# Attention with mixed-in projections: projections that end in period 51 instead of 48, head stacks loaded 16 rounds ahead instead of 20, the rounding of a finished projection moved to the end of a period, and all low weight parts made by GpSimd

## The chip, the core and the metric

The kernel runs on one core of a Trainium2 chip. The metric is the device time of one launch in microseconds (us). The core has five engines with queues of their own: TensorE (PE in the profile; PEld is its weight load), VectorE (DVE), ScalarE (ACT), GpSimd (POOL) and SyncE (SP), which issues most of the DMA transfers. Each engine works through its instructions in the order in which the program gives them, and waits where an input isn't there or a buffer isn't free.

## The reference

Four layers on x of 2048 tokens by 576 features: attention, a spectral filter, attention, a spectral filter. The change lies in the two attention layers, which are the same but for their inputs:

```python
def _A_ref(x, wqkv, wo):
    B, S, D = x.shape
    H = 32; Dh = D // H; W = 256
    qkv = (x @ wqkv).reshape(B, S, 3, H, Dh).transpose(2, 0, 3, 1, 4)
    q, k, v = qkv[0], qkv[1], qkv[2]
    scores = jnp.einsum("bhqd,bhkd->bhqk", q, k) * (Dh ** -0.5)
    idx = jnp.arange(S)
    mask = (idx[:, None] - idx[None, :] >= 0) & (idx[:, None] - idx[None, :] < W)
    scores = jnp.where(mask[None, None], scores, -1e9)
    p = _softmax(scores, axis=-1)
    o = jnp.einsum("bhqk,bhkd->bhqd", p, v)
    return o.transpose(0, 2, 1, 3).reshape(B, S, D) @ wo

x = x + _A_ref(_layernorm(x), A_wqkv, A_wo)
x = x + _B_ref(_layernorm(x), B_w_r, B_w_i)   # filter by rfft2 and irfft2
```

So there are 32 heads of 18 features, and each token sees itself and the 255 tokens before it.

## The kernel before

**Precision.** Every product is taken with operands split into a high part, rounded to fp32r, and a low remainder. That is why the code has pairs such as `wh` and `wl`, and why a projected q or k is written out as two parts.

**Projections.** The 1152 columns of q and k are nine blocks of 128 (`i`), and the 2048 tokens four chunks of 512 (`c`). One block with one chunk is a *unit*: 14 steps of matmul (`k_steps`). In the mixed part each step is two matmuls, one on each half of PE's rows, into two PSUM banks `pj` and `pk`. When a unit's last step is done, four things follow: ACT copies both banks into an SBUF tile `sg` (line 1129); `total` adds them on POOL (line 1133); `high` rounds the sum on ACT (line 1136); `remainder` takes the low part on POOL (line 1142); and `send` stores both parts, 512 KB, in the DRAM tensor `qk_d` with a DMA from SP's queue (line 1145). There are two `sg` tiles, taken in turn.

**Stacks.** The heads are done in eight groups of four (`n`, `NQ = 8`). A group's q and k stand in SBUF as a *stack*: two tiles `qs` and `ks`, which hold the parts in slots one above the other so that one matmul gives the sum of the products. Even groups use one pair of tiles and odd groups the other. `stack_load` (line 1162) fills one chunk of 512 tokens of a stack from `qk_d`, and a quarter of a chunk takes three DMAs of 72 KB. The quarters 0 and 1 fill `qs`, 2 and 3 `ks`.

**Rounds and periods.** One round `t` handles one tile of 128 keys or queries of one group, for its four heads; 16 rounds are a group and 128 rounds the layer. Ten rounds ahead (`LEAD = 10`) the maximum of each query's scores is found: a matmul `S` (line 1187) and one DVE instruction with the mask, followed by a short read of its accumulator (line 1189). In `m_rows` four tiles' maxima are turned by PE (`tpm`, line 1199), negated by ACT (`mt`, line 1201) and put by two small DMAs of SP (line 1203) into a spare row of `qs`; the matmul `E` (line 1219) then gives scores that are already lowered by the maximum, and ACT takes their exponential into `P` (line 1220). Two selects of POOL (lines 1222 and 1225) clear what the mask excludes.

Two rounds are a *period* `p`, and `mixed()` writes 59 of them (`MIX = 118`). A period has first its block of eight `S` and eight `E` matmuls with the projection steps between them, and at its end the *value block*: 32 small matmuls `U` of `P` with v (line 1240; 16 of them where a group begins), which DVE then transposes (line 1246). Ahead of the value block stand the actions planned in `end`; odd periods also have an `m_rows` behind it. Even periods have a transpose `back` (line 1270) and odd ones a reciprocal (line 1261) on DVE. `early` actions are written behind the first `S` of a period, `mid` actions after its first round. A `U` shares three PSUM banks with the `E` matmuls, so it takes over the bank of the sixth `E` of its period and starts only when ACT is done with that one.

**What sets the order.** All of it is written out by hand. `ends` says in which period each of the 23 units of the mixed part is finished (the earlier ones are done in an opening part): with `1 + 47 * u // 22` in periods 1 to 48, most of them two periods apart and seven steps in each. Periods that have no step are filled with 14 small matmuls on an identity (`warmpj`, `warmpk`). `loads(t)` says which quarter of which stack is loaded in round `t`.

**Weights of the next product.** In the last periods (`behind`) the output weights are loaded in five pieces, and `out.split(k)` makes the high part on ACT (line 751) and the low part by a subtraction (line 752): on POOL for the first three pieces and on DVE for the last two. `OB` is 120.

After period 58 a short tail does the remaining ten rounds (exponentials and values only), and then the product with the output weights begins.

## Time and profile before

| what | us |
|---|---|
| median of three runs | 1326.73 |
| lowest and highest run | 1315.5, 1673.2 |
| the profiled execution: its time | 1323.85 |
| the profiled execution: its span (first to last instruction) | 1322.1 |
| first attention layer, value block of period 1 to that of period 49 | 249.22 |
| second attention layer, the same stretch | 247.44 |

The page gives for each engine its busy time, for each group of instructions the count, the mean time of one and the idle time ahead of it with what ended it, and the chain of work that ended last. The answers of the trace that are shown below are of these kinds: busy time by stretch; a timeline of one engine, in which a row gives the start in us, the duration, the engine, the line, the instruction with its tiles and shapes, and in square brackets the idle time ahead of it and what ended that. SPq is SyncE's queue of DMA issues. A row whose last column is x4 stands for four instructions in a row.

### The profile page before, as it was taken

What the parts mean: (1) busy time and instruction counts of PE and PEld (TensorE: products, weight loads), DVE (VectorE), ACT (ScalarE), POOL (GpSimd) and SP (SyncE); (2) the same over time, 40 slices, a digit from 0 to 9 for tenths busy, and PEclk for the clock granted to TensorE, in tenths of its full rate; (3) what the DMA queues carried; (4) which work ended last, traced back from release to release, by engine and by line L of the source; (5) the groups of instructions that cost most, each with busy time, mean ns of one, the idle gap of its engine ahead of it and who ended that gap; (6) DMA issues with size and microseconds to landing.
All of it is one profiled execution on the core that took longest, in us unless ns stands there. A gap on an engine that the chain in (4) does not pass through costs nothing.

```text
span 1322.1 us, 35482 instructions
## 1 busy us (share of the span) xinstructions
PE 1281.5 (97%) x12115; PEld 1005.3 (76%) x12115; DVE 956.0 (72%) x3196; ACT 777.0 (59%) x1944; POOL 771.0 (58%) x1248
## 2 busy tenths in 40 slices
PE   8999999999999899999999999999999999899998
PEld 8986666666678699975999976666666686897687
DVE  5417889889899577757674148888889896676755
ACT  5522777878777545533355315777877778473233
POOL 2258777898776443567221196788878767113811
PEclk9999999999999999999999999999999999999999
DMA  6846666665566646688873368576665667498874
GB/s 202 220 153 206 209 199 219 213 213 193 192 199 218 199 120 225 198 261 258 275 264 74 89 204 224 194 212 195 199 199 184 201 207 247 137 346 266 287 237 164
DMA packets 179497, 274.37 MB, mean 208 GB/s; under 512 B 67743, under 2 KB 77727, under 8 KB 177989
## 3 DMA queue, kind: packets, MB, share of 16 engines
q1 hardware_dynamic: 167007, 243.63, 58.7%
q0 software_dynamic: 4656, 13.44, 3.8%
q10 hardware_dynamic: 7654, 15.03, 3.2%
q8 instruction: 97, 1.59, 0.5%
q14 instruction: 83, 0.68, 0.2%
HBM read 164.54 MB, written 114.81 MB: 211 GB/s over the span
## 4 chain that ended last, share of the span: by engine, by line
PE 80%; ACT 6%; DMA 5%; DVE 4%; issue 2%; SPq 1%; POOL 1%; DVEq 0%; ACTq 0%; POOLq 0%
PE U L1240 11%; PE pj L1115 10%; PE vps L1005 9%; PE S L1187 8%; PE ops L802 7%; PE pk L1115 6%; PE E L1219 6%; PE po L274 4%; ACT P L1220 4%; PE pq L524 3%; PE p L503 2%; PE pf L274 2%; PE pi L600 2%; PE pz L312 1%; DMA ks<-qk_d 1%
## 5 line engine op out<-in xcount | busy, mean ns | idle before, releaser
L1189 DVE CUSTOM_DVE_ANT_0 jk<-S,mask 128x384 bf16<-128x384 f32 (+2 forms) x1024 | 482.8, 527 | 35.1 <-PE S L1187 13.3
L1220 ACT ACTIVATE P<-E 128x384 f32<-128x384 f32 (+2 forms) x1024 | 409.3, 487 | 95.4 <-PE E L1219 49.7
L1219 PE MATMUL E<-qs,ks 64*128 64x384 f32 (+2 forms) x1024 | 324.3, 372 | 7.2 <-ACT P L1220 4.5
L1187 PE MATMUL S<-ks,qs 63*128 63x384 f32 (+2 forms) x1024 | 325.0, 370 | 5.6 <-DMA qs<-qk_d 2.7
L1222 POOL TENSOR_SCALAR_AFFINE_SELECT P<-P 128x512 f32<-128x512 f32 x256 | 162.3, 634 | 133.5 <-ACT P L1220 125.3
L1219 PEld LDWEIGHTS E<-qs,ks 64*128 64x128 f32 x1024 | 180.6, 185 | 63.1 <-ACT P L1220 42.1
L1187 PEld LDWEIGHTS S<-ks,qs 63*128 63x128 f32 x1024 | 172.7, 185 | 66.0 <-DVE m L1189 37.8
L1240 PE MATMUL U<-P,vq 128*32 128x256 f32 (+2 forms) x3840 | 185.1, 329 | 0.0
L1240 PEld LDWEIGHTS U<-P,vq 128*32 128x32 f32 (+1 forms) x3840 | 107.1, 109 | 75.4 <-POOL P L1225 16.3
L1115 PE MATMUL pj<-xh,wqh 64*128 64x512 f32 (+1 forms) x360 | 154.9, 430 | 0.0
L1225 POOL TENSOR_SCALAR_AFFINE_SELECT P<-P 128x512 f32<-128x512 f32 x224 | 144.0, 643 | 0.0
L1115 PE MATMUL pj<-xh,wql 64*128 64x512 f32 (+1 forms) x360 | 138.6, 425 | 0.0
L1115 PE MATMUL pj<-xl,wqh 64*128 64x512 f32 (+1 forms) x288 | 120.4, 418 | 0.0
L802 PE MATMUL ops<-oroom 128*128 128x290 f32 (+1 forms) x812 | 114.0, 297 | 1.7 <-DVE ofree L848 1.2
L802 PEld LDWEIGHTS ops<-oroom 128*128 128x128 f32 x812 | 110.4, 189 | 2.3 <-ACT ofree L836 1.5
L1115 PE MATMUL pk<-xh,wqh 64*128 64x512 f32 x230 | 92.2, 401 | 0.0
L1115 PE MATMUL pk<-xh,wql 64*128 64x512 f32 x230 | 91.1, 400 | 0.0
L1246 DVE STREAM_TRANSPOSE us<-U 128x256 f32<-128x256 f32 x128 | 57.1, 446 | 46.6 <-PE U L1240 45.6
L1189 DVE DVE_READ_ACCUMULATOR2_ANT m<- 128x1 f32 x1024 | 84.9, 83 | 0.0
L1115 PE MATMUL pk<-xl,wqh 64*128 64x512 f32 x184 | 73.1, 397 | 0.0
L1115 PEld LDWEIGHTS pj<-xh,wqh 64*128 64x128 f32 (+1 forms) x360 | 66.8, 186 | 7.5 <-issue 1.5
L789 POOL TENSOR_TENSOR oroom<-oraw,oroom 64x128 fp32r<-64x128 f32 x26 | 13.9, 535 | 99.1 <-ACT oroom L787 49.2
(522 smaller groups left out, 2869.6 us busy)
## 6 DMA issues: line engine op xcount, KB each, us to landing
qk_d<-sg SPq DMA_DIRECT2D x56, 512.0 KB
qs<-qk_d SPq DMA_DIRECT2D x384, 72.0 KB
ks<-qk_d SPq DMA_DIRECT2D x348, 72.0 KB
op_d<-o SPq DMA_DIRECT2D x56, 256.0 KB
v_d<-vt SPq DMA_DIRECT2D x32, 304.0 KB
vq<-v_d SPq DMA_DIRECT2D x16, 608.0 KB
wt<-in_w SPq DMA_DIRECT2D x16, 580.0 KB
ofree<-x SPq DMA_DIRECT2D x16, 580.0 KB
```

Source lines behind the costliest of these rows:

```text
L274: T.matmul(ps[:, c, 0:NF], tail[r] if si == 4 else hl_(si), dcs[b // 2][r, b % 2], start=mi == si == 0, stop=si == 4)
L802: self.nc.tensor.matmul(self.ps[u][n][:, 0:self.n], x, self.w[p][:, (2 * wk + n) * self.n:(2 * wk + n + 1) * self.n], start=first and i == ...
L1005: T.matmul(ps[:, n, 0:288], xT(xk, c), w[:, wk, n * 288:(n + 1) * 288], start=i == 0, stop=i == len(ks) - 1)
L1115: T.matmul(ps.rearrange("r (n p) -> r n p", n=NT) if second else ps, w[r, wk], x[r], start=s == 0, stop=s == len(ks) - 1)
L1187: T.matmul(ps[:, 0:N], q[b:b + 63, pair, i * 128:i * 128 + 128], k[b:b + 63, pair, lo:hi], start=True, stop=True)
L1189: V.tensor_tensor_reduce(out=jk[:, 0:N], in0=ps[:, 0:N], in1=mask[:, 384 - N:384], scale=1.0, scalar=-3e38, op0=ALU.add, op1=ALU.max, accu ...
L1219: T.matmul(ps[:, 0:nq], k[b:b + 64, pair, j * 128:j * 128 + 128], q[b:b + 64, pair, j * 128:j * 128 + nq], start=True, stop=True)
L1220: A.activation(p[:, hl_, 0:nq], ps[:, 0:nq], AF.Exp, scale=SC)
L1222: P.affine_select(out=p[:, :, 0:128], in_=p[:, :, 0:128], pattern=[[0, 4], [1, 128]], compare_op=ALU.is_ge, fill=0.0, base=0, channel_mult ...
L1225: P.affine_select(out=p[:, :, 256:384], in_=p[:, :, 256:384], pattern=[[0, 4], [-1, 128]], compare_op=ALU.is_gt, fill=0.0, base=0, channel ...
L1240: T.matmul(U[32 * h:32 * h + v.shape[1], (q0 - e) * 128:(q1 - e) * 128], v, pt[n, j][:, h, (q0 - j) * 128:(q1 - j) * 128], start=j == max( ...
L1246: V.transpose(us[n, c][:, 8 * k:8 * k + 8].rearrange("r b (a p) -> r (b a) p", a=2), U[:, 0:256].rearrange("r (p n) -> r n p", n=NT))
```

## The change

Four edits, in `split`, `loads`, `mixed` and `behind`:

- The units end by `1 + 50 * u // 22`: in periods 1 to 51, so that periods 0 to 51 hold steps instead of 0 to 48. Six units take three periods where three did before, and seven periods of a layer have the filling matmuls instead of ten.
- From round 4 on, one quarter of a stack is loaded in each round: the stack that is next, chunk by chunk. Before, stack 2's first chunk was loaded in rounds 12 to 15 beside the last chunk of stack 1, and from then on everything came four rounds earlier than now. The number of loads is the same.
- `high` goes from the middle of the period after the unit's end to the end of that period, ahead of the value block. `remainder` goes from that middle to the beginning of the next period, and `send` from the middle of that next period to its end.
- All five low weight parts are made by POOL, and every split comes two rounds earlier.

```diff
     def split(self, k):
         c = slice(2 * self.n * k, 2 * self.n * (k + 1))
         self.nc.scalar.copy(self.w["h"][:, c], self.raw[:, c])
-        (self.nc.vector if k > 2 else self.nc.gpsimd).tensor_sub(self.w["l"][:, c], self.raw[:, c], self.w["h"][:, c].bitcast(F32))
+        self.nc.gpsimd.tensor_sub(self.w["l"][:, c], self.raw[:, c], self.w["h"][:, c].bitcast(F32))
...
-                n, c = divmod(t + (12 if t < 16 else 20), NT)
-                if 4 <= t < 16 or 1 < n < NQ and t >= 12:
-                    stack_load(1 if t < 16 else n, t // 4 if t < 16 else c // 4, (t % 4,))
-                if 12 <= t < 16:
-                    stack_load(2, 0, (t % 4,))
+                n, c = divmod(t, NT)
+                if t >= 4 and n + 1 < NQ:
+                    stack_load(n + 1, c // 4, (t % 4,))
...
-                ends = [1 + 47 * u // 22 for u in range(23)]
+                ends = [1 + 50 * u // 22 for u in range(23)]
...
                     for total, high, remainder, send in ended:
                         total()
-                        for f in (high, remainder):
-                            plan(mid, p + 1, f)
-                        plan(mid, p + 2, send)
+                        plan(end, p + 1, high)
+                        plan(early, p + 2, remainder)
+                        plan(end, p + 2, send)
...
-                if 0 <= t - (OB - 10) < 10 and t % 2 == 0:
-                    out.split((t - (OB - 10)) // 2)
+                if t - OB + 12 in range(0, 10, 2):
+                    out.split((t - OB + 12) // 2)
```

How the instructions stand on two engines shows the edits best. The first place is ACT in period 4 of the first layer, the period after a unit's end: `P_8` and `P_9` are the exponentials of the period's two rounds, `CAST sg` is `high`. Before:

```order
L1201 ACTIVATE mt_3_1991<-tpm_3_1989 16x128
L1220 ACTIVATE P_8_2002<-E_0_2003 128x384
L1220 ACTIVATE P_8_2002<-E_1_2014 128x384
L1220 ACTIVATE P_8_2002<-E_2_2017 128x384
L1220 ACTIVATE P_8_2002<-E_3_2026 128x384
L1136 CAST sg_2_1960<-sg_2_1960 128x512
L1220 ACTIVATE P_9_2048<-E_0_2049 128x384
L1220 ACTIVATE P_9_2048<-E_1_2058 128x384
L1220 ACTIVATE P_9_2048<-E_2_2061 128x384
L1220 ACTIVATE P_9_2048<-E_3_2070 128x384
```

The same place in the changed kernel, down to the first exponential of period 5:

```order
L1201 ACTIVATE mt_3_1991<-tpm_3_1989 16x128
L1220 ACTIVATE P_8_2002<-E_0_2003 128x384
L1220 ACTIVATE P_8_2002<-E_1_2014 128x384
L1220 ACTIVATE P_8_2002<-E_2_2017 128x384
L1220 ACTIVATE P_8_2002<-E_3_2026 128x384
L1220 ACTIVATE P_9_2046<-E_0_2047 128x384
L1220 ACTIVATE P_9_2046<-E_1_2056 128x384
L1220 ACTIVATE P_9_2046<-E_2_2059 128x384
L1220 ACTIVATE P_9_2046<-E_3_2068 128x384
L1136 CAST sg_2_1959<-sg_2_1959 128x512
L1220 ACTIVATE P_10_2109<-E_0_2110 128x384
```

The rounding moved from behind the fourth exponential of its period to behind the eighth.

The second place is SP's queue in periods 5 to 7 of the first layer, from one pair of `mt` rows to the next: `qs_1059` and `ks_1061` belong to stack 1, `qs_1058` and `ks_1060` to stack 2, `op_d<-o` stores finished values. Before:

```order
L1203 DMA qs_1059<-mt_0_2213 2x4x128 x2
L1162 DMA qs_1059<-qk_d 18x2x512 x3
L1162 DMA qs_1058<-qk_d 18x2x512 x3
L1162 DMA qs_1059<-qk_d 18x2x512 x3
L1162 DMA qs_1058<-qk_d 18x2x512 x3
L1162 DMA ks_1061<-qk_d 18x2x512 x3
L1162 DMA ks_1060<-qk_d 18x2x512 x3
L1275 DMA op_d<-o_1_2309 128x512
L1145 DMA qk_d<-sg_3_2182 128x2x512
L1162 DMA ks_1061<-qk_d 18x2x512 x3
L1162 DMA ks_1060<-qk_d 18x2x512 x3
L1203 DMA qs_1059<-mt_1_2445 2x4x128 x2
```

The same stretch in the changed kernel:

```order
L1203 DMA qs_1059<-mt_0_2213 2x4x128 x2
L1162 DMA qs_1059<-qk_d 18x2x512 x6
L1162 DMA ks_1061<-qk_d 18x2x512 x3
L1275 DMA op_d<-o_1_2301 128x512
L1162 DMA ks_1061<-qk_d 18x2x512 x3
L1145 DMA qk_d<-sg_3_2181 128x2x512
L1203 DMA qs_1059<-mt_1_2433 2x4x128 x2
```

Between the two pairs of `mt` rows stand 12 loads instead of 24, and the send has gone from ahead of the last `ks` loads to directly ahead of the `mt` rows.

## The prediction

> **What bounds the kernel now.** I read the page's head and the chain of work that ended last, then the busy time by stretch of the mixed part, then the timelines of TensorE, ScalarE and SyncE's queue at the places that the diff touches.
>
> ```profile
> span 1322.1 us, 35482 instructions
> PE 80%; ACT 6%; DMA 5%; DVE 4%; issue 2%; SPq 1%; POOL 1%; DVEq 0%; ACTq 0%; POOLq 0%
> ...
> core 0: us, PE busy (x) PEld busy (x) DVE busy (x) ACT busy (x) POOL busy (x), PEclk, DMA share, GB/s
> 136.68:385.90 249.22, 244.53 (x2878) 163.93 (x2876) 219.84 (x863) 193.64 (x484) 201.52 (x282) 0.99 0.64 205
> 385.90:425.91 40.01, 39.66 (x598) 32.89 (x596) 36.67 (x145) 28.15 (x73) 26.84 (x42) 1.00 0.64 200
> 813.60:1061.04 247.44, 244.03 (x2878) 163.37 (x2877) 219.63 (x863) 193.32 (x484) 197.40 (x274) 1.00 0.65 199
> ```
>
> The chain puts 80% on PE, but a busy PE is not PE at its peak. The windows run from value block to value block. The first and third cover periods 2 to 49 of the two attention layers, the second the eight periods 50 to 57 without a projection step. Those eight need 40.01 us, 5.00 a period, with DVE busy for 36.67 of it: eight score maxima a period and the transposes around them bound a period that has nothing else to do. The 48 periods before need 5.19 and 5.16 each. So the whole of what the projections cost in time is 249.22 - 6 x 40.01 = 9.2 us in the first layer and 7.3 in the second, and more if periods 50 to 57 have costs of their own (they do, below).
>
> Which periods pay it? The value blocks give each period's length; the pieces are periods 24, 38 with 39, and 52 with 53.
>
> ```profile
> 253.73 1.51 PE L1240 MATMUL U<-P,vq 128*32 128x256 f32 x32
> 258.85 1.51 PE L1240 MATMUL U<-P,vq 128*32 128x256 f32 x32
> ...
> 324.82 1.51 PE L1240 MATMUL U<-P,vq 128*32 128x256 f32 x32
> 330.17 1.51 PE L1240 MATMUL U<-P,vq 128*32 128x256 f32 x32
> 335.03 1.51 PE L1240 MATMUL U<-P,vq 128*32 128x256 f32 x32
> ...
> 395.03 1.51 PE L1240 MATMUL U<-P,vq 128*32 128x256 f32 x32
> 400.13 1.51 PE L1240 MATMUL U<-P,vq 128*32 128x256 f32 x32
> 405.02 1.51 PE L1240 MATMUL U<-P,vq 128*32 128x256 f32 x32
> ```
>
> Even periods carry a transpose more than odd ones, so I compare like with like. Period 24 has seven steps and ends a unit: 258.85 - 253.73 = 5.12. Period 52 has no step: 5.10. Period 38 also has seven steps, and the rounding of the unit that ended in 37: 5.35. Of the odd ones, 39 has seven steps and a unit's end and lasts 4.86, and 53 has nothing and lasts 4.89. Steps and unit ends thus cost about nothing; the period with the rounding costs 0.25. ScalarE's timeline shows how (period 38, then 52):
>
> ```profile
> 325.10 0.66 ACT L1129 COPY sg<-pj 128x512 f32<-128x512 f32 x1
> 325.57 0.69 ACT L1129 COPY sg<-pk 128x512 f32<-128x512 f32 x1
> ...
> 326.98 1.64 ACT L1220 ACTIVATE P<-E 128x384 f32<-128x384 f32 x4
> 328.49 0.63 ACT L1136 CAST sg<-sg 128x512 fp32r<-128x512 f32 x1
> 328.99 1.67 ACT L1220 ACTIVATE P<-E 128x384 f32<-128x384 f32 x4
> 332.12 1.35 ACT L1220 ACTIVATE P<-E 128x256 f32<-128x256 f32 x4 [1.46 <-PE S L1187]
> ...
> 397.25 3.47 ACT L1220 ACTIVATE P<-E 128x384 f32<-128x384 f32 x8 [0.20 <-PE E L1219]
> ```
>
> The cast splits eight exponentials that otherwise run in one piece of 3.47 us, so the sixth, on whose bank the value block waits, is half a microsecond later: two of the last four, 0.84 us, behind 328.99 is 329.83, and the block starts at 330.17. Behind the eighth exponential ACT then has nothing to do for 1.46 us.
>
> **The change part by part.** *Rounding to the period's end.* The cast of 0.63 us goes into that idle 1.46 us, behind the eighth exponential, where nothing of the value block waits for it. There are 23 units in each layer: 46 x 0.25 = 11.5 us. Bounds: no gain, if the delay comes from something that moves along, and all the excess that the windows leave. For that upper end the weights' own cost in periods 50 to 57 has to be taken off: three of those periods hold a copy of 0.7 us in the middle of ACT's exponentials, like the cast, and if each costs 0.3 the bare eight periods are 39.1; 48 of them are 234.6, so the excess without the stall below is 11 us a layer, 22 in all. I take 11.5, which two pairs of rows give directly.
>
> *Remainder and send.* POOL's subtraction keeps its length and moves half a period back:
>
> ```profile
> 330.19 1.28 POOL L1142 TENSOR_TENSOR sg<-sg 128x512 fp32r<-128x512 f32 x1
> ...
> 321.34 0.39 SPq L1145 DMA_DIRECT2D qk_d<-sg  x1
> ...
> 326.86 1.06 SPq L1203 DMA_DIRECT2D qs<-mt  x2
> ```
>
> Behind it on POOL stand the selects of the next round; the value block needs them only a period later, so 1.28 us is hidden; without that cover it would show 46 times. The send moves past three `ks` loads in SP's queue and stands right ahead of the `mt` rows in odd periods. In before it is issued 5.5 us ahead of them, in the change after the remainder, which by my estimate is done 2.5 us into the period (its 1.28 us behind what POOL has left over from the period before), so about 3 us ahead. I cost this at nothing and keep the late `mt` as a rival. The Trainium skill ("DMA: Bandwidth & Descriptors", section "Queues, rings and completion order") says that each DMA engine takes the descriptors of one ring in their order, which would put the small `mt` rows behind all 512 KB of the send; what that would give here is worked out in that rival.
>
> *Loads, one quarter a round.* Rounds 12 to 15 issue half as many loads. What the doubling costs shows in period 9 of each layer:
>
> ```profile
> 157.32 2.43 SPq L1162 DMA_DIRECT2D ks<-qk_d  x3
> ...
> 161.44 4.46 SPq L1162 DMA_DIRECT2D qs<-qk_d  x12
> 165.94 2.95 SPq L1162 DMA_DIRECT2D ks<-qk_d  x6
> ...
> 171.08 3.00 SPq L1162 DMA_DIRECT2D ks<-qk_d  x6
> 174.18 1.49 SPq L1203 DMA_DIRECT2D qs<-mt  x2
> ...
> 163.64 1.51 PE L1240 MATMUL U<-P,vq 128*32 128x256 f32 x32
> ...
> 173.85 1.51 PE L1240 MATMUL U<-P,vq 128*32 128x256 f32 x32
> 176.95 0.41 PE L1187 MATMUL S<-ks,qs 63*128 63x384 f32 x1 [1.59 <-DMA qs<-qk_d]
> 177.61 0.41 PE L1219 MATMUL E<-qs,ks 64*128 64x384 f32 x1 [0.26 <-DMA qs<-mt]
> 182.39 0.86 PE L1240 MATMUL U<-P,vq 128*32 128x256 f32 x16
> ...
> 850.56 1.51 PE L1240 MATMUL U<-P,vq 128*32 128x256 f32 x32
> 857.11 0.86 PE L1240 MATMUL U<-P,vq 128*32 128x256 f32 x16
> ```
>
> SP's queue is so far behind that the last loads of stack 1 are issued until 174.08 and its maxima until 175.67; PE waits for both. Period 9 lasts 182.39 - 173.85 = 8.54 us in the first layer and 6.55 in the second, against 4.86 for an odd period like it: 3.7 + 1.7 = 5.4 us, which go with the 12 extra loads. Bounds 0, if the queue stays behind, and 5.4; I take all, since the removed issues (half of 4.46, 2.95 and 3.00) are 5.2 us of SP's time.
>
> From stack 2 on, each quarter comes four rounds later: the last quarter of a chunk is issued three rounds ahead of its first use. Stack 1 runs so already: its `ks` loads end at 159.75 and are used behind the value block that ends at 165.15, 5.4 us later; PE's wait at 176.95 says that a load lands within 2.9 us of its issue. Cost nothing, with 2.5 us to spare.
>
> *Steps over three more periods.* The steps are the same and cost 0.02 a period by 24 against 52; 84 filling matmuls a launch fall away where the bound is DVE. Nothing.
>
> *Weights on POOL.*
>
> ```profile
> 429.70 0.79 DVE L752 TENSOR_TENSOR oroom<-ofree,oroom 128x576 fp32r<-128x576 f32 x1 [0.32 <-ACT oroom L751]
> ...
> 420.40 1.41 POOL L752 TENSOR_TENSOR oroom<-ofree,oroom 128x576 fp32r<-128x576 f32 x1
> ...
> 420.81 0.56 DVE L1189 CUSTOM_DVE_ANT_0 jk<-S,mask 128x384 bf16<-128x384 f32 x1
> ...
> 435.44 0.67 ACT L751 CAST oroom<-ofree 128x576 fp32r<-128x576 f32 x1
> ```
>
> In period 58 DVE, the bound there, stops for 0.32 + 0.79 = 1.1 us; on POOL the same costs 1.41 of an engine that is busy for 26.84 of 40.01. The fifth copy leaves the tail, where ACT works without a break (about 0.6), and a copy appears in period 54 (about -0.3). At best 1.4 us a layer, at worst a loss of 0.3 if POOL is late with its selects; I take 1.0, so 2 in all. The Trainium skill ("GPSIMD Engine Reference", section "Engine selection") speaks against the move: it rates POOL at about half DVE's speed with two inputs, and the trace agrees, 1.41 to 0.79. The same page's "Key points" has POOL and DVE contend for SBUF when DVE reads two SBUF inputs; the score maximum at 420.81, wholly inside a POOL subtraction, takes 0.56 like others, so the rule does not bite on an instruction with one input from PSUM.
>
> Sum: 11.5 + 5.4 + 0 + 0 + 2 = 18.9 us. The profiled execution took 1323.85, 1.75 more than its span; less 18.9 that is 1305. It lies 2.9 under the median of the runs (1326.73) and inside their spread, the lowest being 1315.5.
>
> **The rivals.**
>
> *All of the excess goes.* Then the first term is its upper end, 22: 1323.85 - 22 - 5.4 - 2 = 1294. For it: periods 39 and 53 show that steps alone are free. Against: splitting the next block's weights puts copies of ACT into the middle of five other periods, and these stay.
>
> *The rounding was not the cause.* PE ends the chain in this part, so the 0.25 might be PE's. Then 7.4 us remain: 1316. Against: period 24 has as many steps and lacks the 0.25.
>
> *Late maxima.* Issued at 326.86 for 1.06 us, `mt` is needed at 331.68, when the block of 330.17 ends: 3.8 us after the second issue. In period 9, right behind 432 KB of loads, it took from 175.67 to 177.61, 1.9. If the send's 524 KB came wholly ahead of it, at the 205 GB/s of the window that is 2.6 us more, 0.7 too late; in the 12 units that end in odd periods, twice: 17 us, so 1322. Against: 3 us of lead.
>
> *Slower: late stacks.* If SP's queue falls behind by more than 2.5 us, the last quarter lands after its use and PE stands, as in period 9. There are 24 chunks a layer in stacks 2 to 7. A wait of 0.4 us at each of the 48 eats the whole gain; the 1.59 of period 9 would make 76 us, 1381; 1 us makes 1353, which is over 2% slower. For it: three rounds of lead instead of seven, with sends ahead in the queue. Against: stack 1 does well with that lead up to round 12.
>
> **How the numbers follow.** The forecast, 1305, has 0.60; all of the excess 0.16; not the cause 0.13; late maxima 0.05; late stacks 0.06. The forecast's own range is 1298 to 1312. Below 1294 and above 1318 I leave out less than 2 in 10: half of the last two cases and a little of the first two. About 2% is what a measurement of this kernel can tell from no change. Faster by that means under 1300: the second case and a tenth of the first, with runs that spread by 1%, 0.24. Slower by that needs late stacks of over 1 us: 0.04. The rest, 0.72, is within 2%.
>
> **What would show it.** Right: the cast stands behind eight unbroken exponentials in the idle time ahead of the next period; period 38's length falls to about 5.10; period 9 to about 4.9, with no wait of `S` for a load; no subtraction of weights on DVE. Wrong: value blocks still 5.35 apart in the periods after a unit's end; `E` waiting for `mt` in odd periods; `S` waiting for `qs` or `ks` at the start of a chunk; ACT idle ahead of the cast, waiting for POOL's sum.

## The result and the profile after

| | before | after |
|---|---|---|
| median of 18 runs each, us | 1324.45 | 1311.88 |
| lowest and highest run | 1315.5, 1673.2 | 1305.8, 1316.8 |
| the profiled execution: its time | 1323.85 | 1312.47 |
| its span | 1322.1 | 1310.7 |

The run of 1673.2 us lies far outside the others and has no trace; the ratio compares fast runs, so it is not in it.

The ratio is 0.9904 with an interval of 0.9888 to 0.992: a gain of 12.6 us, under the 2% that was set as the bound. The forecast was 1305, a gain of 18.9, with a range of 1298 to 1312. The median lies inside that range by 0.1 us, much less than the runs scatter: that it lies inside at all is luck.

The head of the page of the changed kernel and its chain of work that ended last:

```profile
span 1310.7 us, 35140 instructions
...
PE 81%; DMA 9%; DVE 3%; ACT 2%; issue 2%; SPq 1%; POOL 1%; ACTq 0%; DVEq 0%; POOLq 0%
```

ACT went from 6% of the chain to 2%, and DMA from 5% to 9%: something now stands at transfers. The busy time by stretch of the changed kernel says where; its columns are those of the same view in the prediction (length of the stretch, then PE, PEld, DVE, ACT and POOL busy, clock, DMA share, GB/s). The stretches are cut at the same value blocks as there (periods 2 to 49, then 50 to 57), the first two in the first layer, the others in the second:

```profile
134.64:378.15 243.51, 239.14 (x2832) 161.81 (x2831) 217.80 (x863) 194.18 (x480) 200.05 (x279) 0.99 0.64 205
378.15:420.40 42.25, 39.80 (x561) 31.02 (x559) 36.83 (x146) 30.16 (x78) 30.89 (x45) 1.00 0.75 229
806.09:1045.57 239.48, 237.64 (x2833) 159.76 (x2831) 217.35 (x863) 194.19 (x480) 195.72 (x271) 1.00 0.64 200
1045.57:1090.02 44.45, 40.99 (x561) 32.50 (x559) 36.88 (x145) 30.47 (x77) 31.36 (x45) 0.96 0.74 221
```

The 48 periods are 5.7 us shorter in the first layer (249.22 before) and 8.0 in the second (247.44). But the eight periods behind them, which took 40.01 us in the first layer before, now take 42.25 and 44.45.

**What went as forecast.** Here are the value blocks that bound period 38 and period 9 of the first layer in the changed kernel:

```profile
318.81 1.51 PE L1240 MATMUL U<-P,vq 128*32 128x256 f32 x32
323.93 1.51 PE L1240 MATMUL U<-P,vq 128*32 128x256 f32 x32
...
173.61 1.51 PE L1240 MATMUL U<-P,vq 128*32 128x256 f32 x32
178.51 0.86 PE L1240 MATMUL U<-P,vq 128*32 128x256 f32 x16
```

Period 38, which holds a rounding, lasts 323.93 - 318.81 = 5.12 us instead of 5.35. Period 9 lasts 4.90, in the second layer 4.92 (842.96 to 847.88), instead of 8.54 and 6.55. ScalarE's timeline of period 38 shows the cast where the prediction put it:

```profile
320.96 1.64 ACT L1220 ACTIVATE P<-E 128x384 f32<-128x384 f32 x4
322.76 1.74 ACT L1220 ACTIVATE P<-E 128x384 f32<-128x384 f32 x4 [0.16 <-PE E L1219]
324.37 0.63 ACT L1136 CAST sg<-sg 128x512 fp32r<-128x512 f32 x1
```

The eight exponentials run without the cast between them, and the cast starts when the value block has already begun. The periods that hold a rounding can be compared with periods that hold none and stand at the same place of their group of eight. Summed over the 44 of them outside period 2, the time above such a period was 13.6 us before and is 1.7 after.

**What did not.** TensorE's timeline from the value block of period 56 to that of 57, first layer, then second; and VectorE's in the second layer:

```profile
412.91 1.51 PE L1240 MATMUL U<-P,vq 128*32 128x256 f32 x32
416.53 0.41 PE L1187 MATMUL S<-ks,qs 63*128 63x384 f32 x1 [2.12 <-DMA ks<-qk_d]
...
420.40 0.86 PE L1240 MATMUL U<-P,vq 128*32 128x256 f32 x16
...
1080.33 1.51 PE L1240 MATMUL U<-P,vq 128*32 128x256 f32 x32
1085.13 0.49 PE L1187 MATMUL S<-ks,qs 63*128 63x384 f32 x1 [3.29 <-DVE us L1246]
...
1090.02 0.86 PE L1240 MATMUL U<-P,vq 128*32 128x256 f32 x16
...
1083.93 0.71 DVE L1270 STREAM_TRANSPOSE o<-us 128x512 f32<-128x512 f32 x1 [2.90 <-DMA op_d<-o]
```

Period 57 lasts 7.49 us in the first layer and 9.69 in the second, 5.24 in both before. In the first layer PE waits for the last loads of `ks`, those of chunk 3 of stack 7. In the second DVE waits for a store: `o` has one buffer, `back` writes it, and the store that was to empty it has not landed. The transpose of `U` stands behind `back` on DVE, and PE behind that. SyncE's queue in periods 53 to 56 of the first layer shows the place where both come from; the last row is that of the same loads in the second layer:

```profile
397.46 0.46 SPq L1145 DMA_DIRECT2D qk_d<-sg  x1
...
400.54 0.35 SPq L758 DMA_DIRECT2D dc<-dcr  x1
402.81 1.01 SPq L1162 DMA_DIRECT2D qs<-qk_d  x3
403.86 0.36 SPq L744 DMA_DIRECT2D ofree<-in_wo  x1
...
405.77 1.07 SPq L1162 DMA_DIRECT2D ks<-qk_d  x3
407.49 0.36 SPq L744 DMA_DIRECT2D ofree<-in_wo  x1
407.94 0.72 SPq L1275 DMA_DIRECT2D op_d<-o  x1
408.70 2.68 SPq L1162 DMA_DIRECT2D ks<-qk_d  x3
...
1080.07 1.54 SPq L1162 DMA_DIRECT2D ks<-qk_d  x3
```

The last send of the layer goes out at 397.46, in round 107. The loads of round 108 read what it stores: SP stands from 400.89 to 402.81. Two pieces of the weights (288 KB each by the list of DMA issues; one of the expectations below calls them 580 KB) and a second one of the constants (290 KB each) go out among the loads. The store of `o` goes out at 407.94 and lands by 414.77, when `back` starts. The last three `ks` loads begin to go out at 408.70, are issued by 411.38, and have landed by 416.53: 7.8 us behind the first issue and 5.2 behind the last. The prediction had reckoned with 2.9 behind the last. In the second layer they are issued by 1081.61, when the block of period 56 is nearly over (1081.84).

The same happened once in the middle of a layer. Period 21 of the first layer, where chunk 1 of stack 3 is first used, lasts 7.22 us instead of 5.30:

```profile
230.26 1.02 SPq L1162 DMA_DIRECT2D ks<-qk_d  x3
...
235.49 0.41 PE L1187 MATMUL S<-ks,qs 63*128 63x384 f32 x1 [1.65 <-DMA ks<-qk_d]
```

No weights are on the way there; a load of values (608 KB, issued at 222.98) and a send (512 KB, at 224.54) are.

### The profile page after: what moved, and what is told of

Same layout as the page of the kernel before. It is cut to its first block, busy times and chain, and to the rows that moved or that the text cites. A ratio compares the mean times of both kernels' runs of the same rounds, so it can differ in the third digit from the quotient of the medians.

```text
span 1310.7 us, 35140 instructions
## 1 busy us (share of the span) xinstructions
PE 1269.4 (97%) x11947; PEld 997.1 (76%) x11947; DVE 948.1 (72%) x3192; ACT 781.8 (60%) x1944; POOL 777.3 (59%) x1252
## 4 chain that ended last, share of the span: by engine, by line
PE 81%; DMA 9%; DVE 3%; ACT 2%; issue 2%; SPq 1%; POOL 1%; ACTq 0%; DVEq 0%; POOLq 0%
PE pj L1115 12%; PE U L1240 11%; PE vps L1005 9%; PE S L1187 8%; PE pk L1115 8%; PE ops L802 7%; PE E L1219 6%; PE po L274 4%; PE pq L524 3%; PE p L503 2%; PE pf L274 2%; PE pi L600 2%; DMA oraw<-o_d 2%; PE pz L312 2%; DMA qk_d<-sg 1%
## 5 line engine op out<-in xcount | busy, mean ns | idle before, releaser
L1219 PE MATMUL E<-qs,ks 64*128 64x384 f32 (+2 forms) x1024 | 320.2, 371 | 5.9 <-ACT P L1220 4.7
```

What stands on the lines that cost most here:

```text
L1219: T.matmul(ps[:, 0:nq], k[b:b + 64, pair, j * 128:j * 128 + 128], q[b:b + 64, pair, j * 128:j * 128 + nq], start=True, stop=True)
```

## The experiments

Period 57 in the table is that of the first and the second layer in the profiled execution of each kernel. The ratio is to the kernel before, run on the same chip.

| kernel | median us | ratio and interval | period 57, us |
|---|---|---|---|
| `e1_round` | 1309.40 | 0.9918 (0.989 to 0.9946) | 5.24, 5.25 |
| `e2_loads` | 1318.34 | 0.9978 (0.9954 to 1.0002) | 6.90, 5.90 |
| `e3_47` | 1302.79 | 0.9863 (0.9819 to 0.9908) | 5.24, 5.25 |
| `e4_highmid` | 1321.15 | 0.9988 (0.9972 to 1.0004) | 6.36, 6.84 |
| `e5_gradual` | 1309.69 | 0.9896 (0.9853 to 0.9939) | 5.25, 5.25 |
| `e9_last` | 1307.09 | 0.9891 (0.9869 to 0.9914) | 7.05, 6.33 |
| `e7_const` | 1310.94 | 0.9923 (0.9898 to 0.9948) | 7.53, 6.09 |
| `e8_dve` | 1310.97 | 0.9911 (0.9879 to 0.9943) | 7.51, 8.69 |
| `e6_o2` | 1433.53 | 1.0859 (1.0833 to 1.0885) | (periods of 5.9 to 6.4) |
| `e10_weights` | 1311.74 | 0.9933 (0.991 to 0.9957) | 5.64, 5.24 |
| `e12_store` | 1312.63 | 0.9940 (0.9921 to 0.9959) | 9.16, 7.77 |
| `e11_47store` | 1312.12 | 0.9932 (0.991 to 0.9954) | 5.25, 5.70 |

**The rounding, the remainder and the send alone**, added to the kernel before:

```diff
-                        for f in (high, remainder):
-                            plan(mid, p + 1, f)
-                        plan(mid, p + 2, send)
+                        plan(end, p + 1, high)
+                        plan(early, p + 2, remainder)
+                        plan(end, p + 2, send)
```

> The kernel before with the new places of rounding, remainder and send alone. Theory (the cast in the middle of ACT's exponentials held the value block up): the periods after a unit's end fall from about 5.35 to 5.12 us, which is 12 us less over the launch, as in the changed kernel (16.7 us of excess over the periods without steps before, 7.8 after, of which 6.1 is period 2); the stalls of period 9 (3.6 and 1.6 us) stay, and period 57 has none. Time 1311 to 1314. Rival (PE bounds these periods, and the gain came from fewer steps in a period): within 3 us of the kernel before.

It gave a ratio of 0.9918: of 1321.95, the median of before beside it, that is 10.8 us. Period 38 in this kernel:

```profile
319.02 1.51 PE L1240 MATMUL U<-P,vq 128*32 128x256 f32 x32
324.15 1.51 PE L1240 MATMUL U<-P,vq 128*32 128x256 f32 x32
```

5.13 us: nearly the whole term of 11.5 is there, alone. With the old loads, period 9 still stands (6.94 and 8.48 us), now because `E` waits for `mt`:

```profile
176.38 0.41 PE L1219 MATMUL E<-qs,ks 64*128 64x384 f32 x1 [1.72 <-DMA qs<-mt]
```

So a late `mt`, one of the rivals, exists beside the doubled loads; in the changed kernel no `E` waits for it by as much as 0.4 us.

**The loads alone**, added to the kernel before:

```diff
-                n, c = divmod(t + (12 if t < 16 else 20), NT)
...
+                n, c = divmod(t, NT)
+                if t >= 4 and n + 1 < NQ:
+                    stack_load(n + 1, c // 4, (t % 4,))
```

> The kernel before with the loads of one quarter a round alone, 16 rounds ahead. Theory (the shorter lead is what gives time back): the stalls of period 9 go, 5.3 us; period 57 gets a wait of the score matmul for ks, or of DVE for the store of o, of 2 to 4 us in each layer, and period 21 of the first layer one of about 2 us, so that the sum is between 3 us faster and 3 us slower than before. Rival (the new waits come from the late sends and the late end of the projections): no new wait, 5 us faster than before.

Period 9 falls to 4.92 and 4.93, but period 57 gives a part back. TensorE's timeline there, first layer:

```profile
421.80 0.41 PE L1187 MATMUL S<-ks,qs 63*128 63x384 f32 x1 [1.52 <-DMA ks<-qk_d]
```

6.90 and 5.90 against 5.24 is 2.3 us; 5.3 from period 9 less that is 3.0, and by the ratio the kernels differ by 0.0022 x 1321.95 = 2.9 us, though the interval just reaches no change. So the shorter lead costs at the last loads of a layer with the units ending in 48 already.

**The changed kernel with units that end by 47:**

```diff
-                ends = [1 + 50 * u // 22 for u in range(23)]
+                ends = [1 + 47 * u // 22 for u in range(23)]
```

> The changed kernel with the units' ends of before (1 + 47 * u // 22). Theory (the loads that run until round 111 meet the weights and constants in periods 54 and 55): the stall of period 57 stays at 2 us or more, and the time is that of the changed kernel within 2 us. Rival (SP stands at round 108 for the last send, and that makes the last loads late): period 57 falls to about 5.2 us in both layers, 6 us less than the changed kernel. Second rival (spreading the steps saves time by itself): slower than the changed kernel by more than 3 us.

Period 57 is back at 5.24 and 5.25, with no wait for a transfer in periods 54 to 57. The last three `ks` loads and the value block of period 56, first layer:

```profile
405.27 1.83 SPq L1162 DMA_DIRECT2D ks<-qk_d  x3
...
409.98 1.51 PE L1240 MATMUL U<-P,vq 128*32 128x256 f32 x32
```

They are issued 4.71 us ahead of the block of period 56, in the changed kernel 4.21. Its median is the lowest of all, but three of its four runs had a granted clock of 0.997, and the fourth, at 0.992, took 1311.2; what of its lead over the changed kernel belongs to the edit is taken up below.

**The changed kernel with the rounding in the middle of its period again:**

```diff
-                        plan(end, p + 1, high)
+                        plan(mid, p + 1, high)
```

> The changed kernel with the rounding back in the middle of the period after the unit's end; remainder and send stay in their new places. Theory (ACT's cast is the cause): the periods after a unit's end are 0.25 us longer again, some 11 us more than the changed kernel, so about 1323. Rival (POOL's remainder ahead of the second selects was the cause): the same as the changed kernel, within 2 us.

The gain is all but gone (0.9988), and ScalarE's timeline of period 38 has the cast between the exponentials again:

```profile
321.88 1.64 ACT L1220 ACTIVATE P<-E 128x384 f32<-128x384 f32 x4
323.39 0.63 ACT L1136 CAST sg<-sg 128x512 fp32r<-128x512 f32 x1
323.90 1.66 ACT L1220 ACTIVATE P<-E 128x384 f32<-128x384 f32 x4
```

Period 38 lasts 325.08 - 319.73 = 5.35 us in it, to the hundredth what it took before. The cast on ACT was the cause.

**A lead that grows from 16 rounds to 20, with units that end by 47:**

```diff
-                n, c = divmod(t, NT)
-                if t >= 4 and n + 1 < NQ:
-                    stack_load(n + 1, c // 4, (t % 4,))
+                for q in range(*[max(0, s - 4 + min(4, s // 20)) for s in (t, t + 1)]) if t >= 4 else ():
+                    n, c = divmod(q + 4, NT)
+                    if n + 1 < NQ:
+                        stack_load(n + 1, c // 4, (q % 4,))
...
-                ends = [1 + 50 * u // 22 for u in range(23)]
+                ends = [1 + 47 * u // 22 for u in range(23)]
```

> The changed kernel with units that end by 1 + 47 * u // 22 again, and with stack loads whose lead grows from 16 rounds to 20: still one quarter in each round, but one quarter more in every twentieth round until four have been gained. So the doubled rounds 12 to 15 are gone and the last chunks of a stack still come seven rounds ahead of their use from the middle of the layer on. Theory (the doubled loads cost only because they stood in four rounds in a row, and the short lead and the late end cost only in periods 54 to 58): period 9 stays at 4.9 us, period 57 at 5.24 and no period stands at a load; the time is that of the kernel with 47 alone or up to 3 us under it, 1300 to 1304, about 0.984 to 0.986 of before. Rival (each extra quarter costs a stall wherever it stands): four periods near rounds 20, 40, 60 and 80 are 0.5 to 1.5 us longer, the time is 1305 to 1310.

Periods 9 and 57 are clean in both layers (4.93, 5.25). But no gain over `e3_47` came. The time, 1309.69 with a wide interval, is that of the rival, but its mechanism does not show: the periods of rounds 20, 40, 60 and 80 are as long as in `e3_47`. Against that kernel the two profiles differ by 7.5 us in periods 2 to 57; 5.1 of it is period 2, taken up below, and 0.8 is period 25 of the first layer, where `E` waits 1.17 us for `mt`.

**Only the last unit a period earlier:**

```diff
-                ends = [1 + 50 * u // 22 for u in range(23)]
+                ends = [1 + 50 * u // 22 for u in range(22)] + [50]
```

> The changed kernel in which only the last of the 23 units ends one period earlier, in period 50 instead of 51, so that its send is issued two rounds earlier; the other 22 keep their places. Theory 1 (the stall of period 57 comes from the last send: the loads of round 108 wait for it at the head of SP's queue, and all loads, weights and constants behind them are pushed onto each other): SP's gap of 1.9 us ahead of the loads of round 108 goes, the store of op_d and the last ks loads of round 111 are issued some 2 us earlier, and period 57 falls from 7.49 and 9.68 us to 5.3 to 6.5 in both layers: 3 to 6 us less in all, 1306 to 1309. Theory 2 (it is the crowd of transfers alone: weights, constants and loads in the same rounds): period 57 stays within 0.7 us of 7.5 to 9.7 and the time at 1311 to 1313.

SP no longer stands ahead of the loads of round 108, yet period 57 still stands. The last `ks` loads in SP's queue, and PE's wait, first layer:

```profile
408.70 2.55 SPq L1162 DMA_DIRECT2D ks<-qk_d  x3
...
414.89 0.42 PE L1187 MATMUL S<-ks,qs 63*128 63x384 f32 x1 [1.68 <-DMA ks<-qk_d]
```

The excess over 5.24 is 1.81 and 1.09 us here, 2.25 and 4.45 in the changed kernel. The wait for the last send is a part of the cause at most. How far period 57 scatters from run to run is not known, with one trace for each kernel: `e8_dve`, below, leaves all transfers in their places and has 7.51 and 8.69.

**The constants four rounds later:**

```diff
-                if t - OB + 13 in range(0, 10, 2):
-                    out.const((t - OB + 13) // 2)
+                if t - OB + 9 in range(0, 10, 2):
+                    out.const((t - OB + 9) // 2)
```

> The changed kernel with the five loads of constants (dc) four rounds later each, so that two of them leave the rounds 107 to 111 in which the last stack loads are issued. Theory 1 (the last send holds up SP's queue, the constants hardly matter): period 57 falls by less than 1 us in each layer and the time stays at 1310 to 1313. Theory 2 (the crowd of transfers makes the last ks loads and the store of op_d land late): without two of the constants period 57 loses at least half of its excess of 2.25 and 4.44 us, and the time is 1307 to 1310.

Period 57 is as long in the first layer (7.53) and shorter in the second (6.09), and the time is the same. The constants' place does not decide it by itself. Behind the attention layers DVE waits 4.49 and 3.12 us in it for the values that the product reads, in the changed kernel 2.01 and 2.98; whether the later constants are the cause is not shown.

**The low parts of the last two weight pieces on VectorE again:**

```diff
-        self.nc.gpsimd.tensor_sub(self.w["l"][:, c], self.raw[:, c], self.w["h"][:, c].bitcast(F32))
+        (self.nc.vector if k > 2 else self.nc.gpsimd).tensor_sub(self.w["l"][:, c], self.raw[:, c], self.w["h"][:, c].bitcast(F32))
```

> The changed kernel with the low weight parts 3 and 4 subtracted on VectorE again, in the same rounds as in the changed kernel. Theory (the sum's fifth term: VectorE is the bound there): the periods with these two subtractions (56 and 58 or the one behind) are 0.7 to 1.1 us longer each where nothing else holds them, some 1 to 2 us a launch, 1312 to 1315. Rival (the standing of period 57 hides it, or only the earlier round of the split counted and not the engine): the same time within 0.5 us, and the periods 54 to 58 as in the changed kernel.

Period 58 lasts 5.5 us in both layers, 4.80 in the changed kernel: 0.7 a layer, as expected. In the time nothing of it is seen (1310.97, ratio 0.9911). A term of 1.4 us is under what these runs tell.

**Two buffers for `o`, and one for `jk` to make room:**

```diff
-                jk = wp.tile([128, 384], BF, tag="jk", name=f"jk{x}_{pair}_{hp}", bufs=2)
+                jk = wp.tile([128, 384], BF, tag="jk", name=f"jk{x}_{pair}_{hp}", bufs=1)
...
-                    o = wp.tile([128, NT, 32], F32, tag="o", name=f"o{n}_{c}", bufs=1)
+                    o = wp.tile([128, NT, 32], F32, tag="o", name=f"o{n}_{c}", bufs=2)
```

> The changed kernel with two buffers for the tile o, which the store to op_d empties, and in exchange one instead of two for jk, a tile that VectorE's score maxima write and nobody reads. Theory 1 (in period 57 two transfers are late by themselves, the store that empties o and the last ks loads): VectorE no longer waits for the store, neither there nor in the tail (1.15, 2.90 and 1.54 us in the profile of the changed kernel). Period 57 of the second layer, where only the store ended the wait, falls from 9.68 to under 7.5 us; that of the first layer, where S waited longer for ks, stays within 1 us of 7.5. In all 3 to 5 us less: 1306 to 1309. Theory 2 (the store is late because all transfers are, and the ks loads are as late as it): S waits for ks in its place in both layers, period 57 stays over 7 us in both, and the time at 1310 to 1313. If the single jk makes each maximum wait for the one before it, periods without steps are longer than 5.10 and 4.89; that is read off periods 52 and 53.

This told nothing of the store, and much of `jk`. VectorE's timeline late in the first layer:

```profile
456.16 0.56 DVE L1189 CUSTOM_DVE_ANT_0 jk<-S,mask 128x384 bf16<-128x384 f32 x1
...
456.87 0.56 DVE L1189 CUSTOM_DVE_ANT_0 jk<-S,mask 128x384 bf16<-128x384 f32 x1
```

From one maximum to the next it is 0.71 us, in the changed kernel 0.48 (410.06 to 410.54). With one buffer each has to wait until the one before has written the tile, though nobody reads it. Eight in a period make 1.8 us more for the engine that bounds it, and the kernel takes 113 us more than before (1433.53 - 1320.69, the median of before on that chip). In periods of 6 us PE waits for no transfer by more than 0.43 us.

**The weights six rounds later, loads and splits:**

```diff
-                if t - OB + 16 in range(0, 10, 2):
-                    out.weights((t - OB + 16) // 2)
-                if t - OB + 12 in range(0, 10, 2):
-                    out.split((t - OB + 12) // 2)
+                if t - OB + 10 in range(0, 10, 2):
+                    out.weights((t - OB + 10) // 2)
+                if t - OB + 6 in range(0, 10, 2):
+                    out.split((t - OB + 6) // 2)
```

> The changed kernel with the five loads of output weights (580 KB each) and their five splits six rounds later, so that one of the loads instead of three stands among the last stack loads of rounds 104 to 111. Theory 1 (the crowd makes the loads land late: 6 to 8 us from the issue of three to the use, where an uncrowded load lands in about 3): period 57 has no wait for ks or op_d and lasts under 5.6 us in both layers, 6 us less in all; the splits that move into the tail and behind it give 1 to 3 us of that back: 1307 to 1310. Theory 2 (the late place of the loads in SP's queue is enough by itself, whatever else is on the way): period 57 stays over 6.5 us in both layers and the time is 1312 to 1316.

In this kernel the rows of x for the next step are loaded into the buffer of the raw weights two rounds ahead of the splits, so the splits turn x instead of the weights into high and low parts, and ACT waits for those loads in period 58 and the tail; what it says of the tail is therefore worth nothing. Period 57 has no wait for a transfer any more (5.64 and 5.24): the eight periods to it take 39.7 and 39.4 us, against 42.25 and 44.45. The last `ks` loads are issued 5.97 us ahead of the block of period 56 (404.70, 410.67). With the weights later, and all else of the changed kernel in place, the stall is gone.

**The store of `o` half a period earlier**, first in the changed kernel, then together with 47:

```diff
-                            plan(mid, p + 3, store, n, c)
+                            plan(early, p + 3, store, n, c)
```

> The changed kernel with the store of the finished values (op_d from o) planned early in its period instead of in the middle, so that it is issued about 2 us sooner, ahead of the stack loads of its round and as soon as VectorE has written o. Theory 1 (in period 57 the store is late by itself, and in the second layer it alone ends the wait: 2.90 us there, 1.15 in the first layer, 1.54 in its tail): period 57 of the second layer falls from 9.68 us to under 8, the first layer's by less than 1 us since ks still ends the wait there, and the time is 2 to 5 us lower, 1307 to 1310. Theory 2 (what lands late lands late for the sake of the crowd, and an earlier store pushes the ks loads behind it back by as much): period 57 stays over 7 us in both layers, now with S waiting for ks in both, and the time is 1310 to 1314. It could also lose: SP now stands at the head of each odd period until VectorE has written o, and mt rows or loads behind it come later; then periods with a store are longer all through, over 1314.

> Both at once: the changed kernel with units that end by 1 + 47 * u // 22 and with the store of the finished values planned early in its period. With 47 alone no period from 54 to 57 stands, but VectorE waits for that store in the tail, 1.88 us in the first layer and 1.81 in the second. Theory: these two waits go, 1299 to 1302, about 0.983 to 0.985 of before, the fastest of these kernels. Rival (the tail is bound elsewhere, or the store waits for VectorE at the head of SP's queue as long as it gains): the same time as with 47 alone, 1302 to 1305.

With 50, period 57 stands in both layers at `ks` now, by 2.81 and 2.39 us, and is 9.16 and 7.77 long: what the store gained, the loads behind it lost. With 47 the two waits of the tail for the store are gone, and of periods 54 to 58 only 57 of the second layer stands, by less than 0.5 us; but 1312.12 is no gain over 1302.79. From the first run of value matmuls to the last, the two layers of the profiled execution took 310.8 + 309.0 us before, 306.2 + 304.3 in the changed kernel and 300.7 + 301.6 here: 17.5 us less than before. VectorE's timeline behind the last value block of the first layer, of this kernel, and then of `e3_47`:

```profile
441.21 0.43 DVE L787 CAST oroom<-oraw 128x512 fp32r<-128x512 f32 x1 [5.22 <-DMA o_d<-op_d]
```

```profile
437.59 0.43 DVE L787 CAST oroom<-oraw 128x512 fp32r<-128x512 f32 x1 [1.93 <-DMA o_d<-op_d]
```

The product with the output weights needs the packed values (`o_d`) from DRAM. In `e3_47` the last run of value matmuls begins at 436.1 and the product at 441.7; in the changed kernel 440.8 and 446.5. The 4.7 us that the attention ended earlier came through whole. Here the last run begins at 436.5, and the product only at 445.0. SP's queue says why, first of this kernel, then of `e3_47`:

```profile
425.62 0.33 SPq L1275 DMA_DIRECT2D op_d<-o  x1
...
430.75 0.58 SPq L1282 DMA_DIRECT2D o_d<-op_d  x1
431.42 3.10 SPq L1278 DMA_DIRECT2D ofree<-o  x4
...
435.07 0.53 SPq L1282 DMA_DIRECT2D o_d<-op_d  x1
```

```profile
424.39 0.33 SPq L1275 DMA_DIRECT2D op_d<-o  x1
...
426.06 3.67 SPq L1278 DMA_DIRECT2D ofree<-o  x4
429.84 0.55 SPq L1282 DMA_DIRECT2D o_d<-op_d  x1
...
431.06 0.52 SPq L1282 DMA_DIRECT2D o_d<-op_d  x1
```

The edit also moved the stores of the last group (`ofree<-o`) behind the first packing transfer (`o_d<-op_d`, which reads what the store of `o` wrote). In `e3_47` their issue fills the time until that store has landed; here SP stands 4.0 us for the landing, 4.3 in the second layer, and the rest of the packing comes later by about as much. `e12_store` has the same order, with 4.5 and 4.9 us. So both kernels paid for the early store at another place, and their times say little of what it gains.

## Why the prediction was right in kind and 6 us off

**Rounding to the period's end: right.** 11.5 was forecast; the periods that hold it got shorter by 13.6 - 1.7 = 11.9 us, alone it gave 10.8, and with the cast back in the middle the gain was gone. It is nearly the whole result: in the time of the runs, all else in the change together came to nothing (0.9988 in `e4_highmid`).

**Loads, one quarter a round: right.** Period 9 gave 8.54 + 6.55 - 4.90 - 4.92 = 5.3 us of the 5.4 forecast.

**Late loads: here it failed.** The step was "Cost nothing, with 2.5 us to spare": 5.4 us from the end of the last issue to the end of the block behind which the loads are used, less 2.9 us for a load to land, both read in the first periods of a layer. In period 57 of the first layer neither held. The last issue ended at 411.38 and the block at 414.42, which left 3.0 us instead of 5.4; and `S` went on at 416.53, 5.2 us behind the issue instead of 2.9. So the loads were 2.1 us late instead of 2.5 early, half of it by each of the two. In the second layer the issue was later still, 0.2 us ahead of the block's end, though there the landing of the store, not that of the loads, ended the wait. Over the kernels in which `S` waited there for `ks`, it went on 3.6 to 5.5 us behind the last issue.

From the first of the last three issues to the value block of period 56 it was 0.3 to 4.2 us in the kernels that stood there. Where it was 4.7 or more (`e3_47`, `e11_47store`, `e10_weights`), period 57 was at most 0.5 us over 5.24. In the changed kernel the stall costs 2.25 + 4.45 = 6.7 us by the profile, about what is missing of the 18.9. The rival of the late stacks had the mechanism, but spread it over 48 chunks at one price. It struck three: the last chunk of each layer, which shares the queue with the weights of the next product, and chunk 1 of stack 3 in the first layer.

**Steps over three more periods: not nothing.** The steps themselves cost nothing in the three periods. But the last send moves to round 107, a round ahead of the loads that read it. With 47 and all else equal the stall was gone; it went too when the weights were moved and 50 stayed. So the late end alone does not make it, and the crowd without the late end makes a small one at most (2.3 us in `e2_loads`, up to 0.5 in the three later kernels with 47). The send's wait, the constants and the store, each moved alone, did not remove it, and which of them moves SP's queue by how much was not separated further. The Trainium skill ("DMA: Bandwidth & Descriptors", section "Queues, rings and completion order") says that each DMA engine takes one ring's descriptors in order; the trace is in line with it, in that `S` went on at 416.53, behind `back` at 414.77, and the store that `back` waited for had been issued ahead of `ks`. The prediction had used that rule for the small `mt` rows alone.

**Weights on POOL: the size was right, and it can't be seen in the time.** Periods 54, 55, 56 and 58 together took 21.13 us in the first layer before and 20.49 after, and the two tails are 0.4 and 0.5 shorter: with the second layer, which is the same, 2 us. With the subtractions on VectorE again the time was the same.

**Two terms that stood nowhere.** Period 2 took 8.60 and 6.39 us after, 6.10 and 5.80 before, with ACT waiting 2.66 and 1.89 for the landing of a send of the opening part. Among kernels that are the same there it was 4.8 to 8.9, so this belongs to the run and not to the change; in the first layer the block of period 1 had come 2.0 us sooner, which makes up for most of it. Period 21 of the first layer, 1.9 us longer, is the late loads again; with the loads of the changed kernel and the ends of 50 it was 5.3 to 7.2 from trace to trace.

What stays open is the worth of the stall in the whole time. By the profile 47 in place of 50 saves 6.7 us in period 57. By the runs the four kernels without the stall and with the new places of the rounding stand at 0.9863, 0.9896, 0.9932 and 0.9933, the changed one at 0.9904. The last two paid at the other places that were named; a part of the rest lies in the granted clock, below. `e3_47` may be the best of them, but its interval overlaps that of the changed kernel. So the stall is shown in the traces, and that it is what the forecast lacks is not shown by the times.

## What to carry to other kernels

A side task's instruction in the middle of the chain that frees a buffer costs what it delays, not what it lasts: move it behind the last of the chain before looking at its length. A lead has two terms, the time from the last issue to the use and the time to land, and both are to be read where the queue is fullest: here where one phase's last loads meet the next phase's first. A lead that was ample at the start of the layer was short there. And an instruction that is moved in a queue changes its neighbours' places too: look at the whole queue behind it, above all for one that then waits for the moved one to land.

## What the runs showed of the hardware

The scatter of the runs follows the granted clock. On one chip, before ran between 1315.75 us at a mean clock of 0.998 and 1326.61 at 0.991. A straight line through the 144 runs of before, the changed kernel and the experiments but `e6_o2` that list a clock, with a level for each kernel, gives 1.41 us (within 0.18) for each 0.001, and leaves a scatter of 1.8 us. That is about what lost clock would cost if PE were the bound all through: 0.001 of 1310 us is 1.3. Read at a clock of 0.993, before stands at 1323.5, the changed kernel at 1310.6, `e3_47` at 1307.4 and `e11_47store` at 1309.6, the last three within 0.8, 1.9 and 1.2 us. About half of the clock that the changed kernel lost in its profile lies right behind the attention layers. Busy time by stretch there, of before, of the changed kernel and of `e3_47`:

```profile
435.00:500.00 65.00, 60.14 (x546) 52.85 (x539) 43.02 (x117) 32.66 (x89) 28.53 (x54) 1.00 0.50 143
1105.00:1150.00 45.00, 41.31 (x424) 32.61 (x421) 25.28 (x64) 27.07 (x75) 16.48 (x32) 0.96 0.57 174
```

```profile
435.00:500.00 65.00, 60.84 (x507) 56.24 (x508) 44.30 (x121) 28.00 (x78) 26.68 (x53) 0.97 0.50 144
1105.00:1150.00 45.00, 39.97 (x338) 36.00 (x327) 24.26 (x64) 24.90 (x73) 9.89 (x22) 0.92 0.53 157
```

```profile
435.00:500.00 65.00, 60.92 (x484) 58.27 (x477) 46.67 (x123) 25.92 (x73) 25.49 (x53) 0.97 0.51 153
1105.00:1150.00 45.00, 42.95 (x315) 42.54 (x316) 29.50 (x83) 26.23 (x78) 5.55 (x15) 1.00 0.65 212
```

The third number from the right is the clock: 1.00 and 0.96, then 0.97 and 0.92, then 0.97 and 1.00. The mean over all runs, on several chips, was 0.9945 for before and 0.9926 for the changed kernel, 0.9911 and 0.9910 for the two with the early store. Whether a longer wait ahead of the product lowers the clock behind it was not tried.
